# First chunk's attention reordered, weights' steps placed by load: block-sparse attention and MoE on one core

## The chip, the cores and the metric

One core of one Trainium2 chip runs the whole kernel. The metric is the device time of one execution in microseconds (us), median of several runs. The engines named here are TensorE (PE in the profile, PEld for its weight loads), VectorE (DVE), ScalarE (ACT), GpSimd (POOL) and SyncE (SP, which issues most DMAs).

## The reference

```python
# q, k, v: (4, 8, 768, 64) float32; sampled_blocks: (24, 3) int64; block = 32, 24 blocks
scores = (q @ k.T) / 8
mask   = |blk_i - blk_j| <= 1, or either block is the first or the last, or blk_j in sampled_blocks[blk_i]
attn   = softmax(where(mask, scores, -1e9)) (denominator + 1e-9);  x = attn @ v
x      = x.transpose(0, 2, 1, 3).reshape(3072, 512)
h      = x @ w_in                      # (512, 2048)
out    = (h * sigmoid(1.702 * h)) @ w_out   # (2048, 512)
```

The weights arrive as float64 and are turned into float32 on the chip.

## The kernel before, in words

**Units, items, chunks.** Queries are worked in units of 64 rows of one batch (two inner blocks, 11 units, "sparse"; and the first and last block together, one unit, "dense"). The order is: for two batches at a time, units u = 0 to 10 of both, then their dense units. A sparse unit is one item, a dense one four. Eight units make a chunk of 512 tokens (`CU`), and there are six chunks (`NC`). The MoE runs chunk by chunk in 16 ticks each (`NF`, one tick per 128 columns of `w_in`), 96 in all.

**An item.** `scores` issues 32 small matmuls (L260) into two banks, then for each of two heads two minima on VectorE (L283, a tensor-tensor-reduce that also adds the mask) and two exponentials on ScalarE (L288), into `ex`, of which there are four tiles, so those of one item. `transposes` (L303) transposes them on TensorE into banks 3 and 7 (in the early part) and copies each bank to `pt` on ScalarE (L307); behind the copies VectorE computes the factors of the softmax (L357, L358). `values` (L328) issues 64 matmuls with `pt` and V, and VectorE normalises the result into `x` (L370, one buffer). `turn` transposes `x` (L381), and ScalarE writes `xhi` (L388), VectorE `xlo` (L389): the two float32r parts that the MoE reads.

**Loads.** Two items (both batches of one u) share a K entry (q, three window blocks, the one behind them, six sampled blocks of K; L187 to L198) and a V entry (`vmid` L214, two indirect loads `vown` L216). There are two buffers of each (`RING`), and `loads` (L220) issues the next entry as soon as the items that use the buffer have been issued. SP issues most; in the early part POOL issues three of the K blocks, and always `vown`.

**Weights.** `weights` (L395) is a generator that turns 32 float64 tiles (16 of `w_in`, 16 of `w_out`, in turn) into float32 and splits them. Each call is one step, a tile has four: shift (L443, DVE; and it issues the DMA of the tile after next, L411, on ScalarE's queue); the low part of the tile before (L424, DVE) and for a `w_out` tile its save to DRAM (`ws`, L430, on ScalarE's queue); sign (L449, DVE) and the next tile's activation (L419, ACT); low bits (L453, DVE) and the high part (L456, ACT). The tile `a` has three buffers, so L419 of a tile waits for the save of three tiles earlier. `w_out` is held in a ring of three (`WRING`), so a step that would run too far ahead of the `down` matmuls does nothing (L438). Later chunks read `ws` back.

**The order of work.** `first` (L640) does the attention of chunk 0 alone, in ten turns n: values of item n-2, scores of n (with minima and exponentials of each head), two weights' steps, turn of n-2, transposes of n-1 (copies, factors), loads, two weights' steps (the steps from n = 2 on). Then `run` (L664) goes through the ticks. A tick m (L606) is: low part of the last gate (L510), `up` (12 matmuls, L488 to L490, into bank 7), n0 weights' steps, `gate` (tanh on ACT L496, multiply on DVE L497, which reads bank 7 and so frees it), `down` of tick m-1 (L532, L533; L528), in between the high part (L502), then n1 weights' steps; n0 = 4 and n1 = 3 in the first 16 ticks. Each tick has four quarters (q = 4m to 4m + 3), and at each quarter `begin` issues the parts that `plan` (L570) has put there for the next chunk's items: an item's scores at q, its transposes four quarters later (two for dense), with the next item's scores the values of the item before, with the next item's transposes the turn of the item before. For chunk 1, whose items are all sparse, the scores stand at q = 0, 6, 14, 20, 28, 34, 42, 48; those of chunk 2 begin at 56. When a part stands at the third quarter its copies, minima and exponentials are issued behind the gate, at the others at once.

Of the kernel before, what the change touches and what calls it, by code (L numbers as in the profile page):

```python
# [27 lines left out]
NF = DF // P  # L28
NU = (NB - 2) // 2
UT = 2 * BLK  # L30
CU = 8
# [6 lines left out]
QT = 4  # L38
# [5 lines left out]
class Kernel:  # L44
# [57 lines left out]
    def indices(self):  # L102
# [7 lines left out]
        def take(shape):  # L110
            n = 1
            for k in shape:
# [8 lines left out]

        vblk = take([NB])
        first, second = slice(1, NB - 2, 2), slice(2, NB - 1, 2)
        nc.gpsimd.iota(vblk[3 * BLK:P, first], pattern=[[2, NU]], base=0, channel_multiplier=0,
                       allow_small_or_imprecise_dtypes=True)
# [20 lines left out]
        for i in range(NR):  # L146
            for cols, rows in ((first, slice(BLK * i, BLK * (i + 1))), (second, slice(BLK * (i + 1), BLK * (i + 2)))):
                nc.vector.tensor_copy(out=vblk[rows, cols], in_=sbw[rows, cols, i])
# [95 lines left out]
    def scores(self, g):  # L244
        nc, un, sparse = self.nc, g["unit"], self.sparse(g)
        r = g["k"]["n"] % RING
        g["k"]["scores"] -= 1
        if g["first"]:
            un["rs"] = self.small.tile([P, 2, NPAIR], F32, name="rs")
            un["nm"] = self.small.tile([P, 2, NPAIR], F32, name="nm")  # L250
        sps = self.psum("s", g["n"])
        if sparse:
            bi, n = un["b"] % 2, 2 * P
            kg = self.kg[r][:, :, bi].rearrange("p n (a s) -> p n a s", a=NPAIR)
            for i in range(2):
                for a in range(2):
                    for j in range(2):
                        for h in range(2):
                            pair, rows, c = 2 * i + a, slice(D * h, D * (h + 1)), 2 * a + j
                            nc.tensor.matmul(  # L260
                                sps[h][BLK * c:BLK * (c + 1), n * i:n * (i + 1)].rearrange("p (n s) -> p n s", s=BLK),
                                self.qt[r][rows, bi, UT * pair + BLK * j:UT * pair + BLK * (j + 1)],
                                kg[rows, 4 * j:4 * j + 8, pair], start=True, stop=True, tile_position=(D * h, BLK * c))
            parts = [(i, 0) for i in range(2)]
            bias = self.bias[:, un["u"]].rearrange("p (n o) -> p n o", o=1).broadcast_to([P, 8, BLK])
        else:
            kt = self.kg[r].rearrange("p n b c -> p (n b c)").rearrange("p (a s) -> p a s", a=NPAIR)
            i, half, n = g["i"], g["half"], S // 2
            for a in range(2):
                for h in range(2):  # L270
                    pair, rows = 2 * i + a, slice(D * h, D * (h + 1))
                    nc.tensor.matmul(sps[h][UT * a:UT * (a + 1), 0:n], self.qt[r][rows, 0, UT * pair:UT * (pair + 1)],  # L272
                                     kt[rows, pair, n * half:n * (half + 1)], start=True, stop=True, tile_position=(D * h, UT * a))
            parts = [(i, half)]
            bias = self.zero.broadcast_to([P, n])
        g["ex"] = {}

        def of(h):
            for k, (i, half) in enumerate(parts):
                at = sps[h][:, n * k:n * (k + 1)]  # L280
                if sparse:
                    at = at.rearrange("p (n s) -> p n s", s=BLK)
                nc.vector.tensor_tensor_reduce(out=at, in0=at, in1=bias, scale=-SCALE, scalar=3.0e38, op0=ALU.add, op1=ALU.min,  # L283
                                               accum_out=un["nm"][:, half, 2 * i + h:2 * i + h + 1])
            for k, (i, half) in enumerate(parts):
                c = 2 * i + h
                ex = g["ex"][h, k] = self.work.tile([P, 384], F32, name="ex", bufs=4)[:, 0:n]
                nc.scalar.activation(out=ex, in_=sps[h][:, n * k:n * (k + 1)], func=AF.Exp, bias=un["nm"][:, half, c:c + 1],  # L288
                                     scale=-1.0, accum_out=un["rs"][:, half, c:c + 1])

        return [lambda h=h: of(h) for h in range(2)]

    def transposes(self, g):

# [100 lines left out]
    def weights(self):  # L395
# [38 lines left out]
        fetch(1)  # L434
        yield
        first(0)
        for k, (f, i) in enumerate(todo):
            while i == 1 and f - WRING > self.downs - 1:  # L438
# [131 lines left out]
    def plan(self):  # L570

        chunks = [[g for g in self.items if g["unit"]["n"] // CU == c] for c in range(NC)]
        at, starts = {}, []
        for c in range(1, NC):
            begin = 0 if c == 1 else 4 * QT * (4 * c - 4) - 8
            end = 4 * QT * 4 * c - 8
            dense = sum(not self.sparse(g) for g in chunks[c])
            room, count = end - begin - 4 * dense, len(chunks[c]) - dense
            even = 2 if room >= 7 * count else 1
            for k, g in enumerate(chunks[c]):  # L580
                q = room * k // count // even * even if self.sparse(g) else room + 4 * (k - count)
                starts.append((begin + q, g))
        starts.append((end, None))
        put = lambda q, part, g: at.setdefault(q, []).append((part, g))
        for k, (q, g) in enumerate(starts):
            before = starts[k - 1][1] if k else None
            turn = q + 4
            if g is not None:
                put(q, self.scores, g)
                turn = q + (4 if self.sparse(g) else 2)  # L590
                put(turn, self.transposes, g)
            if before is not None:
                put(q, self.values, before)
                if before["end"]:
                    put(turn, self.turn, before)
        return at
# [6 lines left out]
        self.loads()  # L603
        return after

    def tick(self, m, n0, n1):  # L606


        def run(n):
            for _ in range(n):  # L610
                next(self.conv, None)

        def finish(todo):
            for f in todo:
                f()

        moe = m < NC * NF
        self.gate_lo(m - 1)
        finish(self.begin(QT * m))
        if moe:  # L620
            self.up(m, range(0, 2))
        finish(self.begin(QT * m + 1))
        if moe:
            self.up(m, range(2, 4))
        run(n0)
        after = self.begin(QT * m + 2)
        if moe:
            self.gate(m)
        finish(after[:2])
        self.down(m - LAG, 0)  # L630
        if moe:
            self.gate_hi(m)
        finish(after[2:])
        finish(self.begin(QT * m + 3))
        self.down(m - LAG, 1)
        self.split(m + 1)
        self.stream(m + 3)
        run(n1)

    def first(self):  # L640

        items = [g for g in self.items if g["unit"]["n"] < CU]
        at = lambda n: items[n] if 0 <= n < len(items) else None

        def run(part, g):
            for f in part(g) if g is not None else ():
                f()

        def weights(n, k):
            for _ in range(k if n > 1 else 0):  # L650
                next(self.conv)

        for n in range(len(items) + 2):
            if n == 1:
                next(self.conv)
            run(self.values, at(n - 2))
            run(self.scores, at(n))
            weights(n, 2)
            run(self.turn, at(n - 2))
            run(self.transposes, at(n - 1))  # L660
            self.loads()
            weights(n, 2)

    def run(self):  # L664
        self.g, self.wst, self.downs = {}, {}, 0
        self.conv = self.weights()
        self.indices()
        self.loads()
        self.first()
        self.early = False  # L670
        self.at = self.plan()
        for m in range(NC * NF + LAG):
            if m == NF:
                for _ in self.conv:
                    pass
            self.tick(m, 4 if m < NF else 0, 3 if m < NF else 0)


@with_exitstack
# [47 lines left out]
```

## Time and profile before

| | us |
|---|---|
| median of 3 runs | 808.59 (804.4 to 809.12) |
| the profiled execution | 807.86 |
| its span, first to last instruction | 806.2 |

All times of rows are us from the start of that span, of one execution. "Busy" is the time in which an engine works; matmuls are pipelined, so a busy TensorE need not be at its peak. The granted clock is TensorE's share of its full speed.

### The profile page before, as it was taken

The page shows a single profiled execution, that of the slowest core. Times are in us where ns is not written, and L with a number is a line of the kernel's source. Part 1 is how long each engine was busy: PE and PEld are TensorE (multiplying, and loading weights), DVE is VectorE, ACT ScalarE, POOL GpSimd, SP SyncE. Part 2 cuts the span into 40 slices and gives each one's busy share as a digit, 9 for nine tenths or more (in the row PEclk, how much of TensorE's full clock was granted, in tenths as well). Part 3 has the DMA queues.
Part 4 walks back from the last instruction along what each step waited for, and adds up shares of the span by engine and source line. Part 5 has one row for each costly group of instructions (what it writes and reads, how often), then busy time and mean ns, then how long its engine had stood idle before and what let it go on. Part 6 is the DMA issues. An engine that isn't in the chain of part 4 may idle for free.

```text
span 806.2 us, 19246 instructions
## 1 busy us (share of the span) xinstructions
PE 747.6 (93%) x7584; PEld 577.3 (72%) x7584; DVE 414.2 (51%) x1076; ACT 376.7 (47%) x937; POOL 58.1 (7%) x85
## 2 busy tenths in 40 slices
PE   2656898998899999999999999999999999999996
PEld 1434686776677777777877878778777777788885
DVE  3365677877665444455444454444555444443332
ACT  0464455656555444454445454444455444333232
POOL 5032110110000000000000000000000000000000
PEclk9996899999999999999999999999999999999999
DMA  8877687867574344755535455354574222131112
GB/s 263 263 248 257 218 257 223 253 222 223 201 217 166 111 145 126 234 145 169 154 108 162 126 172 162 113 173 129 158 244 157 86 72 74 40 91 53 52 41 52
DMA packets 61116, 128.21 MB, mean 159 GB/s; under 512 B 7569, under 2 KB 26514, under 8 KB 60514
## 3 DMA queue, kind: packets, MB, share of 16 engines
q1 hardware_dynamic: 46882, 80.50, 33.6%
q0 software_dynamic: 7232, 25.51, 9.6%
q10 hardware_dynamic: 6912, 20.97, 8.2%
q8 instruction: 60, 0.98, 0.5%
q14 instruction: 30, 0.25, 0.1%
HBM read 116.47 MB, written 10.49 MB: 157 GB/s over the span
## 4 chain that ended last, share of the span: by engine, by line
PE 77%; DVE 7%; ACT 6%; DMA 4%; issue 3%; ACTq 1%; SPq 1%; DVEq 0%
PE bank L488 11%; PE bank L532 10%; PE bank L490 9%; PE bank L533 9%; PE bank L528 9%; PE bank L489 9%; PE bank L328 5%; PE bank L260 5%; PE bank L303 5%; DMA ws<-a 2%; DMA vmid<-in_v_dram 2%; ACT ex L288 2%; PE bank L336 2%; PE bank L272 2%; DVE a L453 1%
## 5 line engine op out<-in xcount | busy, mean ns | idle before, releaser
L497 DVE SCALAR_TENSOR_TENSOR g<-g,bank 128x512 f32<-128x512 f32 x96 | 66.0, 687 | 198.6 <-ACT g L496 198.6
L488 PE MATMUL bank<-xhi,win 128*128 128x512 f32 x384 | 158.4, 412 | 9.5 <-DVE g L497 8.4
L288 ACT ACTIVATE ex<-bank,nm 128x256 f32<-128x256 f32 (+1 forms) x208 | 99.5, 488 | 143.9 <-DVE nm L283 123.4
L532 PE MATMUL bank<-wout,ghi 128*128 128x512 f32 x384 | 154.7, 403 | 0.0
L533 PE MATMUL bank<-wout,ghi 128*128 128x512 f32 x384 | 151.7, 395 | 0.0
L490 PE MATMUL bank<-xhi,win 128*128 128x512 f32 x384 | 151.2, 394 | 0.0
L489 PE MATMUL bank<-xlo,win 128*128 128x512 f32 x384 | 150.2, 391 | 0.0
L496 ACT ACTIVATE g<-bank 128x512 f32<-128x512 f32 x96 | 57.4, 597 | 148.2 <-PE bank L490 144.9
L528 PE MATMUL bank<-wout,glo 128*128 128x512 f32 x384 | 107.7, 394 | 0.0
L477 DVE TENSOR_TENSOR wout<-wst,wout 128x512 fp32r<-128x512 f32 x80 | 55.4, 692 | 79.7 <-ACT wout L476 78.7
L488 PEld LDWEIGHTS bank<-xhi,win 128*128 128x128 f32 x384 | 72.1, 188 | 28.8 <-DVE g L497 11.1
L283 DVE CUSTOM_DVE_ANT_1 bank<-bank,bias 128x256 f32<-128x256 f32 x176 | 73.8, 440 | 26.0 <-PE bank L260 23.0
L528 PEld LDWEIGHTS bank<-wout,glo 128*128 128x128 f32 x384 | 72.4, 189 | 17.2
L490 PEld LDWEIGHTS bank<-xhi,win 128*128 128x128 f32 x384 | 72.2, 188 | 16.4
L502 ACT CAST ghi<-g 128x512 fp32r<-128x512 f32 x96 | 59.7, 622 | 51.7 <-DVE g L497 51.7
L532 PEld LDWEIGHTS bank<-wout,ghi 128*128 128x128 f32 x384 | 72.2, 188 | 16.0
L533 PEld LDWEIGHTS bank<-wout,ghi 128*128 128x128 f32 x384 | 72.5, 189 | 15.4
L489 PEld LDWEIGHTS bank<-xlo,win 128*128 128x128 f32 x384 | 72.4, 189 | 13.4 <-DVE xlo L389 0.3
L216 POOL DMA_INDIRECT vown<-in_v_dram,vidx x44 | 44.9, 1019 | 480.8 <-PE bank L328 368.4
L328 PEld LDWEIGHTS bank<-vown,pt 128*32 128x32 f32 x1408 | 46.2, 116 | 39.8 <-ACT pt L307 16.6
L260 PE MATMUL bank<-kg,qt 64*32 64x256 f32 x1408 | 57.2, 426 | 18.4 <-DMA kg<-in_kb_dram 11.0
L328 PE MATMUL bank<-vown,pt 128*32 128x64 f32 x1408 | 55.6, 232 | 20.0 <-ACT pt L307 12.3
(73 smaller groups left out, 823.0 us busy)
## 6 DMA issues: line engine op xcount, KB each, us to landing
wst<-ws SPq DMA_DIRECT2D x80, 256.0 KB
kg<-in_kb_dram SPq DMA_DIRECT2D x136, 128.0 KB
kg<-in_kb_dram SPq DMA_DIRECT2D x22, 384.0 KB
raw<-in_moe_w_in_dram ACTq DMA_DIRECT2D x16, 512.0 KB
raw<-in_moe_w_out_dram ACTq DMA_DIRECT2D x16, 512.0 KB
kg<-in_kT_dram SPq DMA_DIRECT2D x4, 1536.0 KB
vown<-in_vd_dram SPq DMA_DIRECT2D x8, 768.0 KB
qt<-in_q_dram SPq DMA_DIRECT2D x22, 256.0 KB
```

The source lines that it names most:

```text
L260: nc.tensor.matmul(sps[h][BLK * c:BLK * (c + 1), n * i:n * (i + 1)].rearrange("p (n s) -> p n s", s=BLK), self.qt[r][rows, bi, UT * pair + ...
L283: nc.vector.tensor_tensor_reduce(out=at, in0=at, in1=bias, scale=-SCALE, scalar=3.0e38, op0=ALU.add, op1=ALU.min, accum_out=un["nm"][:, ha ...
L288: nc.scalar.activation(out=ex, in_=sps[h][:, n * k:n * (k + 1)], func=AF.Exp, bias=un["nm"][:, half, c:c + 1], scale=-1.0, accum_out=un["r ...
L328: nc.tensor.matmul(av[BLK * c:BLK * (c + 1), 0, 2 * i + h], g["pt"][h][:, 2 * i + k, BLK * c:BLK * (c + 1)], src[:, at:at + D], start=(k = ...
L488: nc.tensor.matmul(h, wih[:, k], hi[:, k], start=(k == 0), stop=False)
L489: nc.tensor.matmul(h, wih[:, k], lo[:, k], start=False, stop=False)
L490: nc.tensor.matmul(h, wil[:, k], hi[:, k], start=False, stop=(k == NCT - 1))
L497: nc.vector.scalar_tensor_tensor(out=g, in0=g, scalar=1.0, in1=self.h, op0=ALU.add, op1=ALU.mult)
L502: self.nc.scalar.copy(out=ghi, in_=self.g[m][0])
L528: nc.tensor.matmul(o[n], glo[:, tk[n]], woh, start=False, stop=last)
L532: nc.tensor.matmul(o[n], ghi[:, tk[n]], woh, start=(f == 0), stop=False)
L533: nc.tensor.matmul(o[n], ghi[:, tk[n]], wol, start=False, stop=False)
```

## The change

In `first` the minima of both heads are issued right behind the scores; the exponentials of an item come behind the copies of the transposes of the item before; the values of item n-1 are issued in turn n (before: in turn n+1), ahead of the loads and of the second pair of weights' steps. The loop has nine turns: the ninth does the scores of item 8, the first of chunk 1, and the turn of item 7 closes it. 28 weights' steps stand in it from n = 2 on (before 32), beside the one at n = 1.

In `plan` chunk 1 begins at q = -4 (its first scores are done already), and its sparse items stand every eight quarters until the end asks for six: -4, 4, 12, 20, 28, 36, 44, 50. For the other chunks the places come out as before. In `tick` the weights' steps follow the tick: none ahead of the gate and five at the end in a tick with scores, four and five in another. The steps of the first 16 ticks are 108 (before 112).

```diff
-        def of(h):
+        def least(h):
             for k, (i, half) in enumerate(parts):
...
+        def exps(h):
             for k, (i, half) in enumerate(parts):
                 c = 2 * i + h
...
-        return [lambda h=h: of(h) for h in range(2)]
+        return [lambda h=h: (least(h), exps(h)) for h in range(2)] if not self.early else [
+            lambda: [least(h) for h in range(2)], lambda: [exps(h) for h in range(2)]]
...
-            begin = 0 if c == 1 else 4 * QT * (4 * c - 4) - 8
+            begin = -4 if c == 1 else 4 * QT * (4 * c - 4) - 8
             end = 4 * QT * 4 * c - 8
             dense = sum(not self.sparse(g) for g in chunks[c])
             room, count = end - begin - 4 * dense, len(chunks[c]) - dense
-            even = 2 if room >= 7 * count else 1
             for k, g in enumerate(chunks[c]):
-                q = room * k // count // even * even if self.sparse(g) else room + 4 * (k - count)
+                q = room + 4 * (k - count)
+                if self.sparse(g):
+                    q = min(8 * k, room - 6 * (count - k)) if room >= 7 * count else room * k // count
                 starts.append((begin + q, g))
...
             if g is not None:
-                put(q, self.scores, g)
+                if q >= 0:
+                    put(q, self.scores, g)
...
-    def tick(self, m, n0, n1):
+    def tick(self, m):
+        n0, n1 = 0, 0
+        if m < NF:
+            heavy = any(part == self.scores for q in range(QT) for part, g in self.at.get(QT * m + q, ()))
+            n0, n1 = (0, 5) if heavy else (4, 5)
...
-        for n in range(len(items) + 2):
+        for n, g in enumerate(items):
             if n == 1:
                 next(self.conv)
-            run(self.values, at(n - 2))
-            run(self.scores, at(n))
-            weights(n, 2)
-            run(self.turn, at(n - 2))
-            run(self.transposes, at(n - 1))
+            exps = self.scores(g)
+            exps.pop(0)()
+            if n > 1:
+                weights(2)
+                finish(self.turn(items[n - 2]))
+            if n > 0:
+                finish(self.transposes(items[n - 1]))
+            finish(exps)
+            if n > 0:
+                finish(self.values(items[n - 1]))
             self.loads()
-            weights(n, 2)
+            if n > 1:
+                weights(2)
+        finish(self.turn(items[CU - 1]))
+        self.loads()
...
-            self.tick(m, 4 if m < NF else 0, 3 if m < NF else 0)
+            self.tick(m)
```

## Rows read from the trace of the kernel before

**Rows 1.** The page's first part: busy us, share of the span, instructions.

```profile
PE 747.6 (93%) x7584; PEld 577.3 (72%) x7584; DVE 414.2 (51%) x1076; ACT 376.7 (47%) x937; POOL 58.1 (7%) x85
```

**Rows 2.** Busy time by stretch, with instructions, granted clock, DMA share and GB/s.

```profile
41.00:88.40 47.40, 29.46 (x600) 20.05 (x598) 28.29 (x84) 24.89 (x72) 13.47 (x16) 0.78 0.83 268
88.40:220.70 132.30, 121.18 (x1325) 92.11 (x1325) 101.49 (x245) 76.07 (x186) 9.32 (x8) 0.99 0.70 222
220.70:806.20 585.50, 578.17 (x5380) 452.75 (x5380) 269.17 (x678) 264.32 (x647) 22.50 (x24) 1.00 0.43 129
```

**Rows 3.** Timeline of TensorE, the first MoE matmul: start, us, what, [idle before].

```profile
88.43 0.49 PE L488 MATMUL bank<-xhi,win 128*128 128x512 f32 x1 [1.04 <-ACT xhi L388]
```

**Rows 4.** Busy time by stretch, six turns of the first chunk (PE, PEld, DVE, ACT, POOL).

```profile
28.20:37.40 9.20, 6.46 (x110) 4.97 (x110) 4.48 (x15) 4.90 (x14) 0.00 (x0) 1.00 0.74 245
...
71.00:79.30 8.30, 5.67 (x92) 3.60 (x90) 5.12 (x16) 4.36 (x14) 4.01 (x5) 0.71 0.79 259
sum 51.10, PE 32.67 PEld 22.26 DVE 29.87 ACT 26.61 POOL 11.95; mean PE 5.44 PEld 3.71 DVE 4.98 ACT 4.43 POOL 1.99
```

**Rows 5.** Waits of TensorE, 28 to 88.5 us: total, times, longest.

```profile
PE bank L328 <- ACT pt L307: 12.3, 4, 3.3
PE bank L328 <- ACT xhi L388: 4.6, 2, 2.4
```

**Rows 6.** Timeline of ScalarE in one turn.

```profile
49.46 0.47 ACT L288 ACTIVATE ex<-bank,nm 128x256 f32<-128x256 f32 x1 [4.11 <-PE bank L303]
...
52.08 1.10 ACT L307 COPY pt<-bank 128x512 f32<-128x512 f32 x2
```

**Rows 7.** Waits of VectorE, 28.2 to 79.3 us.

```profile
DVE xlo L389 <- ACT xhi L388: 4.2, 5, 0.8
```

**Rows 8.** The page's DMA issues: KB of each.

```profile
kg<-in_kb_dram SPq DMA_DIRECT2D x136, 128.0 KB
...
raw<-in_moe_w_in_dram ACTq DMA_DIRECT2D x16, 512.0 KB
```

**Rows 9.** Busy time by stretch of 5 us: a quiet and a full one for DMA.

```profile
35.00:40.00 5.00, 4.55 (x100) 3.09 (x101) 2.78 (x10) 1.50 (x3) 0.27 (x1) 1.00 0.51 166
...
60.00:65.00 5.00, 4.42 (x99) 2.64 (x100) 1.89 (x7) 0.97 (x2) 1.34 (x2) 0.66 0.97 329
```

**Rows 10.** Busy time by stretch: two ticks of a later chunk with one item.

```profile
365.50:380.00 14.50, 14.50 (x163) 11.46 (x155) 6.82 (x21) 6.77 (x17) 1.87 (x2) 1.00 0.50 145
```

**Rows 11.** Waits of TensorE, 88.4 to 220.7 us.

```profile
PE bank L488 <- DVE g L497: 8.3, 9, 3.1
PE bank L260 <- ACT pt L307: 2.2, 2, 1.2
```

**Rows 12.** Timeline of ScalarE in a tick with scores; TensorE at ticks 6 and 13.

```profile
132.41 0.62 ACT L456 CAST wout<-a 128x512 fp32r<-128x512 f32 x1 [0.89 <-DVE a L453]
132.94 0.59 ACT L496 ACTIVATE g<-bank 128x512 f32<-128x512 f32 x1
...
134.30 0.50 PE L488 MATMUL bank<-xhi,win 128*128 128x512 f32 x1 [0.80 <-DVE g L497]
...
192.45 0.50 PE L488 MATMUL bank<-xhi,win 128*128 128x512 f32 x1 [0.20 <-DVE g L497]
```

**Rows 13.** Timeline of ScalarE and TensorE at 209 us; busy time by stretch there.

```profile
208.93 0.66 ACT L419 ACTIVATE a<-raw 128x512 f32<-128x512 f32 x1 [2.51 <-DMA ws<-a]
209.49 0.59 ACT L496 ACTIVATE g<-bank 128x512 f32<-128x512 f32 x1
...
210.86 0.50 PE L488 MATMUL bank<-xhi,win 128*128 128x512 f32 x1 [3.08 <-DVE g L497]
...
200.00:220.00 20.00, 16.38 (x177) 12.09 (x166) 14.69 (x39) 10.51 (x29) 2.36 (x2) 0.91 0.54 185
```

**Rows 14.** Waits of VectorE, 88 to 221 us, for its own inputs.

```profile
DVE xlo L389 <- ACT xhi L388: 6.8, 8, 1.4
DVE wout L424 <- ACT wout L456: 2.9, 7, 0.7
```

More of the change, by code (lines that the diff above doesn't have):

```diff
@@ L592, in plan @@
             if before is not None:
+                assert q >= 0
                 put(q, self.values, before)
@@ L640, in first, with finish, weights @@
     def first(self):
[L642 to L650, printed above, removed]
+        items = self.items[:CU + 1]
+        assert items[CU]["unit"]["n"] == CU
+        def finish(todo):
+            while todo:
+                todo.pop(0)()
+        def weights(k):
+            for _ in range(k):
                 next(self.conv)
-        for n in range(len(items) + 2):
+        for n, g in enumerate(items):
             if n == 1:
                 next(self.conv)
-            run(self.values, at(n - 2))
-            run(self.scores, at(n))
-            weights(n, 2)
-            run(self.turn, at(n - 2))
-            run(self.transposes, at(n - 1))
+            exps = self.scores(g)
[8 more added lines that the diff above has]
+                finish(self.values(items[n - 1]))
             self.loads()
-            weights(n, 2)
+            if n > 1:
+                weights(2)
+        finish(self.turn(items[CU - 1]))
+        self.loads()
     def run(self):
```

## The prediction

> **What bounds the kernel now.** I read the page's span and engine shares first: TensorE is busy 93% of the span [rows 1], so the question is where the other 7% lies. The table by stage answers it [rows 2]: from 220.7 us on TensorE is busy 578.2 of 585.5 us, and the change leaves that stretch as it is. The idle time lies in the attention of the first chunk (29.5 busy of 47.4 us between 41 and 88.4) and in the first chunk's MoE (121.2 of 132.3). The first MoE matmul starts at 88.43 us [rows 3]. So the change can win only ahead of that matmul and in the 132.3 us behind it.
>
> In the first chunk one turn of the loop (one item) takes 51.1 / 6 = 8.5 us, in which TensorE works 5.4 us, VectorE 5.0 and ScalarE 4.4 [rows 4] (first and last of six turns, and their sum): none of them is full. What TensorE waits for is named by the waits: 12.3 us for the copies of the transposes (`pt`, L307) and 4.6 us for `xhi` [rows 5]. One turn on ScalarE shows why: the exponentials of item n start when the transposes of n-1 are done (a 4.11 us wait that ends at 49.46), and the copies of those same transposes come behind them, at 52.08 [rows 6]. So 2.6 us lie between finished transposes and their copies, and the values, and the next scores, wait for the copies. Beside this the DMA engines are 0.83 busy from 41 to 88.4, moving 268 GB/s [rows 2]; that is the limit to watch.
>
> **The first chunk, by compute.** The change puts the copies ahead of the exponentials and the values into the same turn. It removes and adds no instruction here except that the scores, minima and exponentials of item 8 stay in front, where they already ran beside the tail, and four weights' steps leave (28 in the loop instead of 32). Per turn the chain scores, transposes, copies, values no longer holds four exponentials, one weights' activation and `xhi`. What is late next is VectorE, which has 5.0 us of work per turn plus 4.2 / 5 = 0.8 us waiting for `xhi` ahead of `xlo` [rows 4, 7]: 5.8 us a turn instead of 8.5. The minima now stand ahead of the weights' steps, `xlo` and the normalisation; all of those are in the 5.0. The stretches of rows 4 are cut where an item's scores start: item 3's start at 37.4 and, without the exponentials ahead of the copies, 2.6 us earlier [rows 6], 34.8. Five turns of 5.8 bring item 8's scores to 63.8. They take about 1.4 us (a quarter of TensorE's 5.4), and the last `xlo`, which the first MoE step reads, closes one more VectorE turn of 5.8: 71.0. By compute the first MoE matmul starts there instead of at 88.4. Item 8's transposes, which move ahead of it, lie in TensorE's idle time there.
>
> **The first chunk, by loads.** A K entry (two items) is ten blocks of 128 KB [rows 8] and, by the shape of its tile, 256 KB of q: 1.54 MB; a V entry is, by its tiles' shapes, 0.25 + 2 x 0.51 = 1.28 MB; a weight tile is 0.51 MB [rows 8]. Between 41 us and the first MoE matmul the changed kernel needs two K entries, two V entries, about five weight tiles and two saves: 3.07 + 2.56 + 2.56 + 0.51 = 8.7 MB, and I add 1.6 MB for prefetches that share the engines with them: 10.3 MB. Before, 47.4 us x 268 GB/s = 12.7 MB went by. At 268 / 0.83 = 323 GB/s, all engines busy, 10.3 MB take 31.9 us and end at 72.9; at the share of before (0.83) 38.4 us, 79.4. Shares of 0.51 and 0.97 both occur [rows 9]: the quiet stretch at 35 to 40 us is one that the earlier V loads (their values come a turn sooner) will fill. I take a share of 0.92, 34.7 us, so about 76 us: 12.4 us won. The bounds are 71.0 (compute alone) and 79.4: 17.4 and 9 us.
>
> A rule of the skill speaks against the larger figure: the Trainium skill (Trainium Kernel Development and Optimization, Key Constraints) says that DMAs issued from the three queues all share the same 16 engines, and several issuers save issue time only. By that rule the loads' order gives no bandwidth, and 72.9 is the floor instead of 71.0; rows 9 agree so far, as three queues together reach 0.97.
>
> **The MoE of the first chunk.** Its TensorE time without stalls comes from later ticks: two ticks with one item are 14.46 us, in which TensorE is full [rows 10]. Here TensorE lost 132.3 - 121.2 = 11.1 us, 8.3 of them in nine waits for the gate's VectorE step (L497) and 2.2 in two waits for `pt` [rows 11]. The step plan changes three things.
>
> First, in a tick with scores no weights' steps stand ahead of the gate. At 130 to 134 us one sees what that removes: the weights' copy (L456) waits for VectorE, the tanh (L496) stands behind it on ScalarE and starts when it is done, and TensorE's next tick waits 0.80 us for the gate; three of the nine waits, 0.80, 1.06 and 0.20, come from such ticks, 2.1 us [rows 12] (the first and the last of the three). Second, the worst one, 3.08 us, comes in the tick that starts the next chunk's first scores: there ScalarE waits 2.51 us for a weights' save (`ws`) with the tanh behind it [rows 13]. With no steps ahead of that gate it goes, and with it the half clock that followed: the granted clock is 0.91 over 20 us, 1.8 us lost [rows 13]. Third, scores move to even places four quarter steps behind the transposes, so one of the two `pt` waits, 1.1 us, goes. Sum: 2.1 + 3.1 + 1.8 + 1.1 = 8.1 us.
>
> Against it: the number of steps a tick is 7 on average in both (5 and 9 now in turn), and all those VectorE instructions stay. VectorE is busy 101.5 us in this stage [rows 2] and waits 6.8 + 2.9 us for its own inputs (`xhi`; the weights' copies) [rows 14]: 111.2 us, or 13.9 per two of the 16 ticks, against TensorE's 14.46. So there is little room to absorb bunches: a tick with nine steps has more of them than its half, and the tick after pays it back. I charge 0.5 us for each of six such pairs, 3 us. Net 5 us won; bounds -3 (all 8.1 stay and the charge comes on top) and +11 (no wait left). Progress of the weights is no issue: the ring of three output weights holds both kernels at the same tile until tick 1, so the four steps fewer cost nothing; only in tick 15 one step is forced by need, under 1 us, in the 3.
>
> **The sum.** 12.4 + 5 = 17.4. The profiled execution took 807.86 us for a span of 806.2, so 807.86 - 17.4 = 790.5 us. That execution lies 0.7 us below the median of 808.59; I leave it there.
>
> **Rivals.** (A, forecast) Loads hold the first chunk at about 76, the stalls half go: 790.5, own range 784 to 797.
>
> (B) Loads don't bind: 71.0, and all 8.1 us of stalls go at no charge: 17.4 + 8.1 = 25.5, 782.4. For it: shares near 1 occur, and turns would have slack. Against: 0.83 is the average already.
>
> (C) The time is given back: loads keep the 0.83 pace (9 us won) and the bunched steps cost what their removal saves, 3 us worse: 6 won, 802. For it: VectorE's 13.9 of 14.46.
>
> (D) The change doesn't do what it says: the exponentials are now behind the copies, so the next transposes wait for them instead, and a turn stays at 8.5; only the missing turn and the stage's stalls help, about 7 us: 801. Against: one ScalarE turn is 4.4 us of work, well under 5.8.
>
> (E) Slower: five steps at the end of each light tick bring the weights' activation (L419) to a save that hasn't landed, and ScalarE, in order, keeps exponentials and tanh behind it, as in rows 13 (3.1 us stall plus 1.8 of clock, 4.9 each). Seven light ticks with one such wait each are 34 us, against 12.4 + 3.2 won elsewhere: 826. From four such waits (19.6) on it is slower. For it: it happened in the looser plan already. Against: only once at that price.
>
> **Chances.** A 0.60, B 0.13, C 0.15, D 0.07, E 0.05. A measurement of this kernel tells about 1%, 8 us: faster is below 800.5, slower above 816.7. A gives 0.57 faster and 0.03 same; B 0.13 faster; C and D 0.06 faster, 0.16 same; E slower: 0.76, 0.19, 0.05. The range 781 to 804 holds B to D and leaves E and the edges out.
>
> **What would show it.** First MoE matmul at 73 to 79 us; turns of 6 to 7 us between successive scores; the `pt` and `xhi` waits of the first chunk (16.9 us) under 6; DMA share there above 0.9. In the MoE behind it a wait for L497 of under 5 us in total, no 3 us one, and 125 to 130 us between first matmuls of ticks 0 and 16. From then on the same row of ticks, 585.5 us to the end. Wrong would be: a first MoE matmul behind 82, long ScalarE waits on `ws`, or a changed length from tick 16 on.

## The result, and the profile after

| | before | after |
|---|---|---|
| median, us (lowest to highest, runs) | 808.86 (804.4 to 809.13, 4) | 796.77 (794.25 to 797.87, 4) |
| the profiled execution, us | 807.86 | 797.87 |
| its span, us | 806.2 | 796.2 |

The ratio is 0.9859, interval 0.9817 to 0.9901: 12 us faster, with an interval clear of 1. The forecast of 790.5 was 6 us too low; the result is inside its range and between rivals A and C.

The busy time by stretch, cut as in [rows 2] (us, then busy time and instructions of PE, PEld, DVE, ACT and POOL, TensorE's granted clock, DMA share, GB/s), of the changed kernel:

```profile
41.00:75.00 34.00, 23.40 (x544) 17.02 (x541) 27.69 (x90) 23.94 (x73) 9.94 (x13) 0.87 0.97 337
75.00:210.00 135.00, 123.18 (x1319) 93.68 (x1319) 101.95 (x240) 76.58 (x180) 8.89 (x8) 0.97 0.71 224
210.00:796.20 586.20, 578.29 (x5381) 452.53 (x5379) 268.04 (x677) 262.87 (x645) 22.48 (x24) 1.00 0.43 128
```

Read against [rows 2]: the first stretch is 34.0 us instead of 47.4, with the DMA engines at 0.97 instead of 0.83. The second, the MoE of the first chunk, has become longer (135 against 132.3), its TensorE as busy within 2 us, its granted clock lower (0.97 against 0.99). The third is the same. So the whole gain lies ahead of the first MoE matmul, and a fifth of it is lost behind it. The stretches are rounded; by the first matmuls themselves they are 75.07, then 134.89 to the first one of tick 16 at 209.96 (before 88.43 and 132.25).

The first MoE matmul in the timeline of TensorE (start, us), to compare with [rows 3]:

```profile
75.07 0.78 PE L491 MATMUL bank<-xhi,win 128*128 128x512 f32 x1
```

Where 1.04 us of waiting stood in front of it, nothing stands now. The waits of TensorE (total us, times, longest) ahead of it, 28 to 75 us, and behind it, 75 to 210 us:

```profile
PE bank L331 <- ACT pt L310: 10.4, 7, 2.3
PE bank L260 <- issue: 3.9, 1, 3.9
...
PE bank L491 <- DVE g L500: 5.6, 6, 1.9
PE bank L260 <- ACT pt L310: 2.9, 2, 1.6
PE bank L536 <- DVE wout L427: 2.2, 1, 2.2
PE bank L306 <- ACT ex L290: 0.5, 2, 0.3
PE bank L493 <- DVE win L427: 0.2, 1, 0.2
```

Ahead of the MoE the `pt` wait is still the largest, 10.4 us (16.9 with `xhi` in [rows 5]). Behind it the waits for the gate fell from 8.3 to 5.6 us [rows 11], but TensorE's idle time in the stretch is 135.0 - 123.2 = 11.8 us, 11.1 before [rows 2]: one list of waits was changed for another of the same length. Two of the new places are worth a look. The first is a tick without scores, with nine steps. Timelines of ScalarE and VectorE and the TensorE matmul that they hold:

```profile
119.45 1.44 ACTq L433 DMA_DIRECT2D ws<-a  x1
120.99 0.68 ACT L422 ACTIVATE a<-raw 128x512 f32<-128x512 f32 x1 [1.36 <-issue]
...
122.25 1.06 ACT L310 COPY pt<-bank 128x512 f32<-128x512 f32 x2
123.20 0.38 ACT L391 CAST xhi<-bank 128x256 fp32r<-128x256 f32 x1
...
126.34 0.62 ACT L459 CAST wout<-a 128x512 fp32r<-128x512 f32 x1 [2.04 <-DVE a L456]
126.87 0.59 ACT L499 ACTIVATE g<-bank 128x512 f32<-128x512 f32 x1
...
123.62 0.42 DVE L392 TENSOR_TENSOR xlo<-bank,xhi 128x256 fp32r<-128x256 f32 x1 [1.03 <-ACT xhi L391]
123.96 0.42 DVE L446 TENSOR_SCALAR a<-a 128x512 int32<-128x512 int32 x1
124.29 0.68 DVE L427 TENSOR_TENSOR win<-a,win 128x512 fp32r<-128x512 f32 x1
124.90 0.69 DVE L452 SCALAR_TENSOR_TENSOR a<-raw,a 128x512 int32<-128x512 int32 x1
125.62 0.69 DVE L456 SCALAR_TENSOR_TENSOR a<-raw,a 128x512 int32<-128x512 int32 x1
127.49 0.69 DVE L500 SCALAR_TENSOR_TENSOR g<-g,bank 128x512 f32<-128x512 f32 x1 [1.18 <-ACT g L499]
...
128.23 0.50 PE L491 MATMUL bank<-xhi,win 128*128 128x512 f32 x1 [1.90 <-DVE g L500]
...
155.40 0.44 ACTq L433 DMA_DIRECT2D ws<-a  x1
...
156.86 0.42 DVE L392 TENSOR_TENSOR xlo<-bank,xhi 128x256 fp32r<-128x256 f32 x1 [1.04 <-ACT xhi L391]
...
161.47 0.71 PE L491 MATMUL bank<-xhi,win 128*128 128x512 f32 x1 [1.91 <-DVE g L500]
```

This is the pattern of [rows 12], the tanh (L499) behind a weights' copy (L459) that waits for VectorE. In the ticks with scores the tanh now stands behind the exponentials alone, and three waits of 0.33 us are left; the pattern stands in the others. `xhi` comes behind the copies of `pt` on ScalarE, VectorE waits 1.03 us for it, four weights' instructions run on VectorE ahead of L459, and the tanh can start only at 126.87. A second wait of 1.91 us, of the same kind, ends at 161.5. The first bunch also holds a save to DRAM (L433) whose issue kept ScalarE for 1.44 us. That is not what makes the wait: ahead of the second one the save's issue took 0.44 us, and the wait is as long.

The second place is tick 15. Timelines of ScalarE, VectorE and TensorE:

```profile
203.77 0.60 ACT L499 ACTIVATE g<-bank 128x512 f32<-128x512 f32 x1
...
204.40 0.69 DVE L500 SCALAR_TENSOR_TENSOR g<-g,bank 128x512 f32<-128x512 f32 x1 [1.38 <-ACT g L499]
205.00 0.68 DVE L427 TENSOR_TENSOR wout<-a,wout 128x512 fp32r<-128x512 f32 x1
...
205.74 0.62 PE L536 MATMUL bank<-wout,ghi 128*128 128x512 f32 x1 [2.15 <-DVE wout L427]
```

And the busy time by stretch, there and at the wait of 161.5:

```profile
157.00:168.00 11.00, 9.09 (x121) 6.73 (x120) 8.41 (x21) 5.70 (x15) 1.87 (x2) 0.84 0.78 266
...
206.00:210.00 4.00, 4.00 (x12) 3.09 (x12) 2.99 (x5) 0.88 (x2) 0.00 (x0) 0.58 0.56 165
```

The second matmuls of `down` wait 2.15 us for the low part of tick 14's output weights (L427). That is the forced step; it takes 0.68 us, but stands on VectorE behind the gate's multiply (L500), which waits 1.38 us for a tanh that stands behind four exponentials on ScalarE. The next 4 us run mostly at the lower clock, 1.2 GHz (0.58 in the mean): 4 x 0.42 = 1.7 us more. At 161.5 it is 11 x 0.16 = 1.8 us in the same way. Before, a wait of 3.08 us stood in front of the same tick, with a clock of 0.91 over 20 us [rows 13]. Between the ticks' first matmuls tick 15 takes 14.2 us; before, it took 9.8.

### The profile page after: what moved, and what is told of

It reads as the page before. It is cut to its first block, busy times and chain, and to the rows that moved or that the text cites. A ratio compares the mean times of both kernels' runs of the same rounds, so it can differ in the third digit from the quotient of the medians.

```text
span 796.2 us, 19245 instructions
## 1 busy us (share of the span) xinstructions
PE 742.6 (93%) x7584; PEld 574.4 (72%) x7584; DVE 413.5 (52%) x1076; ACT 377.4 (47%) x937; POOL 56.6 (7%) x85
## 4 chain that ended last, share of the span: by engine, by line
PE 76%; DVE 9%; ACT 6%; DMA 4%; issue 3%; ACTq 1%; POOL 0%; SPq 0%; POOLq 0%; DVEq 0%
PE bank L491 10%; PE bank L531 10%; PE bank L535 10%; PE bank L536 9%; PE bank L493 9%; PE bank L492 9%; PE bank L306 5%; PE bank L260 4%; PE bank L331 4%; ACT ex L290 2%; DMA ws<-a 2%; PE bank L339 2%; PE bank L272 2%; DVE a L452 2%; DVE a L456 2%
## 5 line engine op out<-in xcount | busy, mean ns | idle before, releaser
L500 DVE SCALAR_TENSOR_TENSOR g<-g,bank 128x512 f32<-128x512 f32 x96 | 66.0, 687 | 199.0 <-ACT g L499 198.9
L536 PE MATMUL bank<-wout,ghi 128*128 128x512 f32 x384 | 152.6, 397 | 2.2 <-DVE wout L427 2.2
L499 ACT ACTIVATE g<-bank 128x512 f32<-128x512 f32 x96 | 57.4, 598 | 145.1 <-PE bank L493 142.0
L536 PEld LDWEIGHTS bank<-wout,ghi 128*128 128x128 f32 x384 | 72.9, 190 | 18.3 <-DVE wout L427 2.6
L216 POOL DMA_INDIRECT vown<-in_v_dram,vidx x44 | 43.3, 984 | 508.8 <-PE bank L331 397.4
L260 PE MATMUL bank<-kg,qt 64*32 64x256 f32 x1408 | 54.8, 409 | 20.4 <-DMA kg<-in_kb_dram 13.6
L310 ACT COPY pt<-bank 128x512 f32<-128x512 f32 (+1 forms) x120 | 61.2, 563 | 20.2 <-PE bank L306 19.7
L513 DVE TENSOR_TENSOR glo<-g,ghi 128x512 fp32r<-128x512 f32 x96 | 65.7, 685 | 1.4 <-ACT ghi L505 1.4
```

Source lines behind the costliest of these rows:

```text
L260: nc.tensor.matmul(sps[h][BLK * c:BLK * (c + 1), n * i:n * (i + 1)].rearrange("p (n s) -> p n s", s=BLK), self.qt[r][rows, bi, UT * pair + ...
L310: copies.append(lambda pt=pt, ps=ps, m=m: nc.scalar.copy(out=pt[:, 0:m], in_=ps[:, 0:m]))
L500: nc.vector.scalar_tensor_tensor(out=g, in0=g, scalar=1.0, in1=self.h, op0=ALU.add, op1=ALU.mult)
L513: self.nc.vector.tensor_tensor(out=glo, in0=g, in1=ghi.bitcast(F32), op=ALU.subtract)
L536: nc.tensor.matmul(o[n], ghi[:, tk[n]], wol, start=False, stop=False)
```

## The experiments

Two theories on the loss behind the first MoE matmul were open (the new places of the scores, or the new split of the steps), and two on the gain ahead of it (the chain over the engines, or the loads). "Stage" below is the time from tick 0's first matmul to tick 16's, 132.25 before and 134.89 after.

**The first chunk's order alone.** The plan and the steps (4 and 3) of before, item 8 back in its chunk:

```diff
-            begin = -4 if c == 1 else 4 * QT * (4 * c - 4) - 8
+            begin = 0 if c == 1 else 4 * QT * (4 * c - 4) - 8
...
-            n0, n1 = (0, 5) if heavy else (4, 5)
+            n0, n1 = 4, 3
...
-        items = self.items[:CU + 1]
+        items = self.items[:CU] + [None]
```

> Only the first chunk's order is the new one (eight items, 28 weights' steps from turn 2 on); places and steps of the first MoE stage are those of before. Theory A (the reorder of the first chunk is the whole gain, the step plan gives nothing or costs): first MoE matmul at 74 to 77 us, the 16 ticks behind it 131 to 134 us, ratio to before 0.980 to 0.988. Rival B (an earlier start needs the step plan, as loads and weights' work crowd the stage): first matmul as early, but the stage 138 us or more, ratio 0.990 to 1.000.

Median 798.22 us against 807.53 (ratio 0.9881, 0.9809 to 0.9952). The first MoE matmul is at 78.11, the stage 132.70; twelve of its 16 ticks are those of before within 0.1 us, the others within 0.7. This is theory A's stage, with a first matmul 1 us behind its range. So the order alone carries about all that the whole change wins: the rest of the change is worth nothing in sum.

**The new plan with the old steps.** Only the split is undone:

```diff
-            n0, n1 = (0, 5) if heavy else (4, 5)
+            n0, n1 = 4, 3
```

> The changed kernel with four and three weights' steps in every tick, as before. Theory A: the stage stays within 132 to 137 us, the ratio to before within 0.003 of the changed kernel's 0.986. Rival B (fewer steps ahead of the gate in ticks with scores do save what was predicted, 5 us, and something else took it back): stage 139 to 143 us, ratio 0.991 to 0.996.

Median 789.75 us (0.9777, 0.9701 to 0.9854): 7 us below the changed kernel, outside what was expected of either. Busy time by stretch and waits of TensorE, 77 to 203.4 us:

```profile
41.00:77.00 36.00, 24.06 (x539) 17.32 (x521) 27.09 (x89) 23.57 (x70) 9.46 (x12) 0.83 0.91 320
77.00:203.40 126.40, 118.42 (x1319) 91.48 (x1317) 100.72 (x237) 75.82 (x179) 7.66 (x8) 0.99 0.75 236
```

```profile
PE bank L491 <- DVE g L500: 6.6, 7, 1.6
PE bank L260 <- ACT pt L310: 1.4, 1, 1.4
```

The stage is 126.4 us, tick 15 8.78. The forced wait of L536 is gone; so is the 3.08 us wait of [rows 13] (the longest is 1.6), though the steps are those of before; and from 79 us on no stretch of this execution runs at the lower clock. The places of the scores and the early item 8 thus win 6.3 us (126.4 against 132.7), and the new split, put on top, costs 5.5 to 8.5 us (131.9 and 134.9 in two profiled executions of the changed kernel).

**Other splits.** Three splits, with the rest as changed: 0 and 7 in every tick; 0 and 6 with scores, 4 and 5 without; 0 and 7 with scores, 4 and 3 without.

```diff
-            n0, n1 = (0, 5) if heavy else (4, 5)
+            n0, n1 = 0, 7
```

```diff
-            n0, n1 = (0, 5) if heavy else (4, 5)
+            n0, n1 = (0, 6) if heavy else (4, 5)
```

```diff
-            n0, n1 = (0, 5) if heavy else (4, 5)
+            n0, n1 = (0, 7) if heavy else (4, 3)
```

> The changed kernel with no step ahead of any gate and seven behind each tick. Theory C (the waits for the gate come from in-order queues: a weights' copy ahead of the tanh): the 5.6 us of waits for the gate and the clock lost behind one of them go, stage 126 to 129 us, ratio 0.977 to 0.981. Rival D (VectorE's total work bounds the stage, wherever the steps stand): the waits move to other instructions, stage 133 to 136 us, ratio 0.984 to 0.988.

Median 798.8 us (0.9891, 0.9819 to 0.9964), stage 135.47. Waits of TensorE behind 76 us:

```profile
PE bank L260 <- ACT pt L310: 6.2, 3, 2.8
PE bank L306 <- ACT ex L290: 3.2, 9, 0.7
PE bank L491 <- DVE g L500: 1.7, 5, 0.3
```

With no step ahead of any gate the wait for the gate does go, 1.7 us against 6.6 with four steps ahead, which is what the change is after; so the order of the steps makes this wait, as theory C has it. The price comes at once in the other waits, 9.4 us: by the order of issue, seven steps in a row stand ahead of the next quarter's minima and copies. The stage is in rival D's range, and the median is worse than either theory gave.

> The changed kernel with six instead of five steps in a tick with scores, so that no step has to be forced in the last tick. If the forced step is what costs there (2.15 us of TensorE's wait in tick 15 and the half clock behind it): tick 15 falls from 14.2 to about 10 us, stage 130 to 132 us, ratio 0.980 to 0.983. If VectorE has no room at all for another step in those ticks, other waits grow as much: stage 134 to 136 us, ratio 0.985 to 0.988.

Median 797.12 us (0.9881, 0.9807 to 0.9955), stage 132.08. Tick 15 is mended (9.28 us), as the first theory has it, and the gain comes back in ticks 4, 8 and 10 (9.7, 9.5 and 10.5 us); the ratio is the second theory's.

> The changed kernel with seven steps in every tick: in ticks with scores all seven behind the tick, in others four ahead of the gate and three behind. Theory H (the plan's idea holds and what cost was the bunch of nine steps in the light ticks and the forced step at the end): stage 122 to 126 us, ratio below 0.978. Rival I (steps moved behind a tick with scores only arrive late at the next tick, which is what cost): stage 129 to 135 us, ratio 0.981 to 0.988.

Median 792.78 us (0.9821, 0.9779 to 0.9863), stage 128.82: the number of steps per tick is seven everywhere, as in the old split, and most of the loss is gone, with the ticks with scores still having none ahead of the gate. The median is rival I's, the stage just under its range; theory H's stage is missed. Waits of TensorE, 75 to 204 us:

```profile
PE bank L491 <- DVE g L500: 6.3, 4, 2.6
```

The waits for the gate are about as long in sum as with four and three steps in every tick (6.6), but two of them, in ticks 6 and 10, are 2.5 and 2.6 us. The changed kernel ran again beside it:

> The changed kernel itself, beside the next three on the same chip: ratio to before 0.984 to 0.989, stage of the first 16 ticks 134 to 136 us with a tick 15 of 13 us or more.

Median 797.08 us (0.9868, 0.9829 to 0.9907), stage 131.91, the first MoE matmul at 77.33; tick 15 takes 12.65 us with a 2.14 us wait of L536, this time with no lower clock behind it. Stage and tick are below what was expected.

**The last ticks alone.** The changed split, but the last two ticks get seven steps:

```diff
             n0, n1 = (0, 5) if heavy else (4, 5)
+            if m >= NF - 2:
+                n0, n1 = (0, 7) if heavy else (4, 3)
```

> The changed kernel with its own split of the weights' steps (0 and 5 in ticks with scores, 4 and 5 in the others), but 0 and 7 in tick 14 and 4 and 3 in tick 15: the last output weights are ready before tick 15's second matmuls ask for them. Theory T (the forced step in tick 15, with the half clock behind it, is most of what the split costs): tick 15 takes 9 to 10 us instead of 12.7 to 14.2, the wait of L536 for the forced last part is gone, the stage from tick 0 to tick 16 is 127 to 130 us, median 791 to 794. Theory B (the bunches of nine steps cost it, and the forced step stands only where they come together): tick 15's gain comes back in ticks 12 to 14, stage 131 to 135, median 795 to 799.

The text says 4 and 3 for tick 15; that tick holds the second scores of chunk 2, so it got 0 and 7, as tick 14 did. Median 795.36 us (0.9845, 0.9796 to 0.9894), stage 130.49. The forced wait is gone and tick 15 takes 10.76 us. The median is only 1.4 to 1.7 us below the changed kernel's, less than the intervals separate, and 5.6 above that of the even steps: theory B's time, with a stage just below its range. The forced step is part of the split's cost, not most of it.

**Fewer steps in the first chunk, eight in ticks 0 to 6.** On top of the even steps:

```diff
-            n0, n1 = 4, 3
+            n0, n1 = 4, 3 + (m < 7)
...
             self.loads()
             if n > 1:
-                weights(2)
+                weights(1)
```

> The kernel with the changed order of the first chunk and even steps, but three weights' steps in a turn of the first chunk instead of four, and the seven steps that this leaves over one each in ticks 0 to 6 (4 and 4 there). That moves about two weight tiles (0.51 MB each) and part of a save out of the first chunk. Theory L (the loads hold the first chunk at some 320 GB/s): 1.1 to 1.3 MB less is 3 to 4 us, first MoE matmul at 72.5 to 74.5 us instead of 77; the stage gives 0 to 3 us back, median 786 to 790. Theory P (compute holds it: the chain over the engines): one step of about 1 us on VectorE or ScalarE less per turn, of which little is on the chain: first MoE matmul at 75 to 77; median 789 to 793.

Median 795.08 us (0.9844, 0.9802 to 0.9887). The first MoE matmul is at 74.57, 2.4 us earlier than with four steps, just behind theory L's range. The stage is 132.77, 6.4 us longer, more than either theory gave, and so is the median. Busy time by stretch, and waits of TensorE, 75 to 207.3 us:

```profile
41.00:74.60 33.60, 22.73 (x541) 17.09 (x524) 24.05 (x81) 21.79 (x69) 9.33 (x12) 0.87 0.91 319
...
PE bank L491 <- DVE g L500: 12.2, 9, 2.4
```

12.2 us against 6.6 with seven steps a tick: seven steps more cost 5.6 us of waiting for the gate, 0.8 us each in the mean of one execution. In the first chunk 33.6 us x 319 GB/s = 10.7 MB went by, against 36 x 320 = 11.5; at 320 GB/s these 0.8 MB take 2.5 us, as much as was won. The seven steps of compute that left with them are not ruled out as its cause.

**The gate's low part on GpSimd.** On top of the even steps, the low part of the gate (L513) goes to GpSimd in the first 16 ticks:

```diff
-        self.nc.vector.tensor_tensor(out=glo, in0=g, in1=ghi.bitcast(F32), op=ALU.subtract)
+        (self.nc.gpsimd if m < NF else self.nc.vector).tensor_tensor(out=glo, in0=g, in1=ghi.bitcast(F32), op=ALU.subtract)
```

> The changed kernel with four and three steps a tick and the gate's low part (L513) of the first 16 ticks on GpSimd instead of VectorE: 16 x 0.69 = 11 us less on VectorE. Theory D (VectorE's total work bounds the stage): stage 120 to 123 us instead of 126.4, ratio 0.970 to 0.974. Rival (waits come from the order of the queues, or GpSimd is too slow for the low part that the down matmuls need): stage 125 us or more.

Median 789.36 us (0.9766, 0.9729 to 0.9803), stage 126.82: no gain over 789.75, and the gate waits stay at 5.9 us. But VectorE was not relieved. Busy time by stretch and groups of instructions, first of the kernel with even steps, then of this run:

```profile
75.00:200.00 125.00, 117.24 (x1314) 91.24 (x1315) 99.48 (x238) 75.36 (x177) 9.17 (x10) 0.99 0.75 235
L446 DVE TENSOR_SCALAR a<-a 128x512 int32<-128x512 int32 x24 | 10.2, 427 | 0.4
...
75.00:200.00 125.00, 116.90 (x1313) 90.43 (x1314) 102.75 (x222) 75.03 (x176) 31.69 (x25) 0.99 0.76 238
L446 DVE TENSOR_SCALAR a<-a 128x512 int32<-128x512 int32 x24 | 15.0, 625 | 0.4
L513 POOL TENSOR_TENSOR glo<-g,ghi 128x512 fp32r<-128x512 f32 x15 | 22.1, 1476 | 84.1 <-ACT ghi L505 84.1
```

The low part left VectorE, and yet VectorE was busy 3.3 us longer (102.75 against 99.48), because its weights' instructions took longer (L446 625 ns in the mean instead of 427). So theory D did not get the test that was meant. What the run shows is the other direction: 3.3 us more of VectorE's work made the stage only 0.4 us longer, and this execution's stage holds a stretch at the lower clock (at 185 us, 1.7 us) that the other's has not. This speaks against VectorE's total as the limit of the stage. That the gate waits for what stands ahead of its tanh and multiply rests on the run with no step ahead of any gate (1.7 us of such waits).

**The loads of the first chunk doubled.** On top of the even steps, each weight tile fetched in the early part is fetched a second time, into DRAM that nobody reads:

```diff
+        self.extra = [dram.tile([P, 2 * DM], I32, name=f"extra{k}") for k in range(12)]
...
+                if self.early:
+                    nc.scalar.dma_start(out=self.extra[k], in_=self.w64[i][NF - 1 - f])
```

> The changed kernel with four and three steps a tick and, in the first chunk only, each weight tile's load issued a second time into a scratch tensor (about ten loads of 0.52 MB that nothing reads). Theory F (with the new order the loads hold the first chunk, DMA share 0.91 to 0.97 there): at some 330 GB/s each takes 1.6 us, first MoE matmul 10 to 16 us later than without, at 87 to 93 us, total 800 to 806. Rival G (the chain over VectorE and ScalarE holds it): at most 4 us later, total under 795.

Median 802.39 us (0.9952, 0.9926 to 0.9978), the first MoE matmul at 91.28, 14.3 us later, as theory F has it; the stage is 123.82. Ten loads of 0.52 MB are 5.2 MB, which at the changed kernel's 337 GB/s take 15.6 us: nearly the full price shows. The page's DMA issues give the number of them, the busy time by stretch the rate:

```profile
extra<-in_moe_w_in_dram ACTq DMA_DIRECT2D x6, 512.0 KB, 6.6
...
extra<-in_moe_w_out_dram ACTq DMA_DIRECT2D x4, 512.0 KB
...
41.00:91.30 50.30, 28.66 (x615) 21.39 (x614) 30.04 (x97) 26.79 (x80) 11.41 (x16) 0.77 0.88 313
```

But the DMA share up to the first MoE matmul is 0.88, not the 0.97 of the changed kernel. ScalarE's waits from 41 to 91 us:

```profile
ACT a L425 <- DMA kg<-in_kb_dram: 12.2, 2, 6.7
ACT a L425 <- DMA qt<-in_q_dram: 2.8, 1, 2.8
```

Ahead of its weights' activations ScalarE stands idle for 15 us, which the profile puts down to K and q loads, and the copies for TensorE come behind them. That is as long as the whole delay. The run shows that more loads cost their time; whether by full DMA engines or by ScalarE held behind a late load it doesn't tell apart.

**The exponentials ahead of the copies again, and the values a turn later.** Both on top of the even steps:

```diff
             exps = self.scores(g)
-            exps.pop(0)()
+            finish(exps)
```

> The kernel with the changed order of the first chunk and the even steps (4 and 3), but with the exponentials of a turn ahead of the copies of the transposes again (minima, exponentials, turn, transposes, copies, values). Theory P (the exponentials ahead of the copies were what held a turn, as the working of the prediction has it: 2.6 us between transposes and copies): five turns are 2 to 2.6 us longer, the loads no longer bind, first MoE matmul at 86 to 89 us instead of 77, median 799 to 803. Theory L (the loads hold the turns, DMA share 0.9 and more; the order only has to be quick enough): part of the 2.6 us is hidden, first MoE matmul at 79 to 84, median 792 to 798. Theory V (it is the values in the same turn that won the time, by freeing V's and K's tiles a turn earlier): first MoE matmul within 2 us of 77, median 788 to 793.

Median 802.49 us (0.994, 0.9919 to 0.9962), the first MoE matmul at 86.07, as theory P has it. The profiled execution, 798.37 us, is the fastest of ten; the medians are 12.7 us apart (789.75 with the copies ahead). Busy time by stretch:

```profile
41.00:86.10 45.10, 27.78 (x605) 20.46 (x605) 28.62 (x91) 25.70 (x77) 9.85 (x13) 0.81 0.76 268
```

The DMA share falls back to 0.76 at 268 GB/s, the rate of before [rows 2]. And the other part:

```diff
             if n > 1:
                 weights(2)
+            if n > 1:
+                finish(self.values(items[n - 2]))
...
-            if n > 0:
-                finish(self.values(items[n - 1]))
...
+        finish(self.values(items[CU - 1]))
```

> The same kernel with copies ahead of the exponentials as in the changed one, but the values of an item a whole turn later, as before the change. Theory P: the turn's chain is as short as in the changed kernel and only the last item's values and turn come later, by one turn's tail: first MoE matmul at 79 to 83 us, median 792 to 797. Theory V: the V tiles come free a turn later, so that the loads behind them start late as before: first MoE matmul at 85 to 89, median 798 to 803.

Median 789.68 us (0.9764, 0.9715 to 0.9814), the first MoE matmul at 76.60: better than either theory gave. Where the values stand is worth nothing; theory V falls. The stage is 127.90 us, with a gate wait of 1.86 us and the lower clock behind it: even steps don't rule that out.

The medians of the kernels with even steps, 789.75, 789.36 and 789.68 us, lie 7 us below the changed kernel and 17 to 18 below the one before. The plain one, the change with its step split undone, is the version to keep.

## Why the prediction was right or wrong

**The first chunk: right in size and in cause.** "12.4 us won" was 13.4 in the profiled execution; the other executions with this order start the first MoE matmul at 75.2 to 78.8. The cause named, exponentials between finished transposes and their copies, is shown: putting them back costs 9.1 us (86.07 against 76.97), and 12.7 us by the medians. The 2.4 us from there to 88.43 belong to the rest of the new order, the four weights' steps that left among it. The early values, which the prediction counted into the shorter chain, contribute nothing. The loads come close behind it, as forecast: the DMA share is 0.97 ("above 0.9"). In other executions with this order it is 0.94 (the changed kernel again), 0.91 (even steps) and 0.85 (the last ticks alone). That the loads are the next limit is likely from this share and from the run with fewer steps, but not shown. The 34.7 us of loading were right by luck, out of two errors that cancel: 34 us at 337 GB/s are 11.5 MB, where the estimate had 10.3 MB at a share of 0.92. Of the 1.2 MB that it lacks, 0.2 are its counting of a KB of the page, which is 1024 bytes, as 1000. Scores follow each other in 6.1 us (35.4 to 65.9 us in five turns), in the "6 to 7".

**The wait that was to show it: wrong.** The `pt` and `xhi` waits were to fall under 6 us; they are 10.4. The prediction took the whole gain out of TensorE's waits. By the stretches, idle time fell from 17.9 to 10.6 us, 7.3 of the 13.4; the other 6.1 is busy time: fewer matmuls lie behind 41 us (544 for 600), and the granted clock there is 0.87 for 0.78. The `pt` line stays the largest, with a DMA share of 0.97: it names where the delay reaches TensorE, and that the loads make it there now is argued from the share, not shown tick by tick.

**The first chunk's MoE: the step that failed.** 8.1 us removed less 3 for bunching were forecast, 5 won; they became 2.6 lost (0.3 won in the second profile). The working was right about which waits would shrink and wrong about what takes their place:

- The three gate waits in ticks with scores, 2.1 us, shrank to three of 0.33. Three of 0.73, 1.90 and 1.91 us came in ticks without scores, with up to nine steps; the other four such ticks have none. The charge for bunching, "0.5 us for each of six such pairs", was 3 us, and these waits are 4.5. It stood on VectorE's total (13.9 us of 14.46; 14.2 with the 2.1 us of waits for `win` that it left out), of which 3.3 us more cost almost nothing in the GpSimd run. Together the gate waits, 5.6 us, are even 1.0 us less than with seven steps in every tick. What the split costs comes by the next points.
- "The worst one, 3.08 us" and the half clock behind it went too, but the credit went to the wrong edit: with even steps and the new places alone no wait stands in front of tick 15, and the longest anywhere is 1.6 us (1.9 in two further executions with these steps, with one stretch at the lower clock in each). The split brought both back in tick 15: 2.15 us for the forced step and 1.7 for the clock.
- "Only in tick 15 one step is forced by need, under 1 us, in the 3": the step was counted rightly and mis-sized. Nine of the 16 ticks have scores, tick 15 too. By the kernel's code 96 of the changed split's steps take effect ahead of tick 15's `down`, which needs 97 (with even steps there are 97), so exactly one is forced. The wait measured 2.15 us, because the step comes behind the exponentials, the tanh and the gate's multiply of that tick. Tick 15 as a whole is 5.4 us longer than with even steps (14.2 against 8.8): this wait, 1.7 us of lower clock, and 1.3 us of waiting for `pt`.
- The lower clock takes 1.8 + 1.7 = 3.5 us of the changed kernel's stage (at 162 and 206 us, each behind a wait of about 2 us); the prediction counted 1.8 us of it as removed and none as added.

The 8.5 us between the two stages (134.9 and 126.4) are 2.2 for the forced wait, 1.5 more for `pt` ahead of scores, 0.7 for `ex` and `win`, 3.5 of clock, less 1.0 for the gate; some 1.6 us stay unassigned. In the second profile of the changed kernel the difference is 5.5.

**The rest: right.** 586.3 us from tick 16 on (585.4 in the second profile) against 585.5.

**The rivals.** C ("bunched steps cost what their removal saves") is what happened in the stage, A ahead of it. E's mechanism, ScalarE held by a `ws` save, occurs twice in the stage for 2.6 us in all, far from its four times 4.9. B fell with the stage, D with the turn of 6.1 us.

## What to carry to other kernels

When two engines hand a tile back and forth in a loop, put the copy that the next engine waits for ahead of work that only the next turn needs; here 2.6 us per turn between a finished transpose and its copy were worth 9 us in the profiles and 12.7 in the medians, with the loads close behind as the next limit. Filler work was best spread evenly over ticks whose main engine is full: even steps took 789.75 us, five other splits 792.78 to 798.8. Bunching it by the "load" of a tick took waits out of one tick and made longer ones in others. After such a change count the filler delivered up to each deadline, the last one above all, and look at what stands ahead of a piece that comes late: its wait can be a multiple of its own length (2.15 us for a step of 0.68).

## What was not expected of the hardware

Issuing a save on ScalarE's queue took 0.61 us at 49.04 us in the changed kernel's trace; at 119.45 it took 1.44 us, and ScalarE did nothing beside it. What it waited for is not shown by a run here.

TensorE's clock fell to its lower level behind waits of about 2 us in some executions and not in others: of the two light ticks with a wait of 1.9 us, 126 and 160 us in the changed kernel, only the second was followed by it, and tick 15's 2.15 us was followed by it in one profile of the changed kernel and not in the other. In other runs a wait of 1.83 us was followed by it (the low part on GpSimd, at 184 us) and one of 2.54 us was not (0 and 7 with scores, 4 and 3 without, at 127 us), so the length of the wait alone doesn't decide it. Each time it cost about 1.7 us, nearly as much as the wait itself.

VectorE's instructions took longer while GpSimd worked on `glo` (L513). In that run, L446 took 952 ns in the mean where it overlapped L513 and 428 ns where it did not, and L452 took 1342 and 683. Moving one instruction of 0.69 us a tick to GpSimd, which needed 1.48 us for it, made VectorE busier.
